# Zero-tile matmuls in TensorE's first waits, reordered loads, the expert number first on VectorE, and batch 0's routing moved into its own MoE stream

## The chip, the cores and the metric

The kernel runs on one core of a Trainium2 chip. A core has TensorE (PE, matrix multiplication; its weight loads are listed as PEld), VectorE (DVE), ScalarE (ACT), GpSimd (POOL), SyncE (SP, which here only issues DMAs) and 16 DMA engines. The metric is device time in microseconds (us) from start to end, as a median over runs. The profile is a record of one such execution.

## The reference

Attention twice over, then two mixture-of-experts (MoE) layers. Batch 8, 8 heads, 576 positions, head size 64, 32 packs; 512 model columns, 8 experts, hidden size 1024, all in float32.

```python
def sm_attn(qq, kk, vv):
    s = scale * np.matmul(qq, kk.transpose(0, 1, 3, 2))
    s = s - np.max(s, axis=-1, keepdims=True)
    a = np.exp(s)
    a = a / (np.sum(a, axis=-1, keepdims=True) + 1e-09)
    return np.matmul(a, vv)
p_packed = sm_attn(p, k, v)
x = sm_attn(q, p_packed, p_packed)      # then 4608 tokens x 512
...
expert_idx = np.argmax(x @ w_gate, axis=1)      # MoE 1
for e in range(E):
    h = np.maximum(x[mask] @ w1[e], 0.0)
    out[mask] = gate_w[mask, None] * (h @ w2[e])
...
# MoE 2: the same with a skip score: tokens with x @ w_skip <= 0 stay as they are
```

## The kernel before

Each batch runs through three generators of the attention: `gen_S` (scores s1 of the packs p against k, their maxima mx, the exponentials a, transposes at, the product pv with v, and the packed keys PKT), `gen_T` (scores s2 of q against PKT in two halves T0 and T1 of 288 positions, softmax along 32 packs, transposed back into A2; also the number e1i of the batch's main expert, from the key sums ks), and `gen_R` (gate logits L and the routing, whose gate rows gT go to DRAM and come back broadcast as gB).

MoE 1 then uses the batch's main expert. `gen_pre` loads that expert's W1 (four tiles of 512 KB, W1c; for batch 0 the last two lie in batch 0's result tile y), forms Q1 = PKT x W1 by matmuls q, and splits Q1 and A2 into a high and a low part (Q1h, Q1l, A2h, A2l) for three-product matmuls. `gen_w2` loads W2 (four tiles of 512 KB, W2c) and splits it into W2h (ACT) and W2l (DVE for tiles 0 and 2 of batch 0, else POOL). `gen_M` is the main stream of TensorE: for each half of the positions, `stage1` makes h in eight blocks of six matmuls (ACT writes hh, DVE writes hl from the same PSUM bank), and `stage2` makes y in four tiles of 24 matmuls; `sink` multiplies each y tile by gB on DVE. `stage2` reads the blocks in the order 3, 2, 1, 0, 7, 6, 5, 4, so the first 12 matmuls of a tile need blocks 0 to 3 alone.

Each engine's instructions stand in one fixed order, which is that in which the program issues them. `merge` takes turns among generators by a string of letters (`PAT`), and `Weave` lets side generators run between the steps of a main one: each side has a number of steps and a stretch of the main stream, as (generator, steps, from, to). Before batch 0's main stream, the attention of batch 0 and part of batch 1's `gen_S`, batch 0's `gen_T`, the first steps of `gen_pre` and `gen_w2`, then all of `gen_R(0)` and the rest of `gen_pre(0)` are issued. Batch 0's W2 tiles 2 and 3 are loaded when the tiles 0 and 1 have been split, since the pool `wcp` has two buffers. All PSUM tiles come from one ring of eight banks.

Of the kernel before, what the change touches and what calls it, by code (L numbers as in the profile page):

```python
# [9 lines left out]
F32 = mybir.dt.float32  # L10
# [12 lines left out]
F = 1024  # L23
# [8 lines left out]
PAT = (  # L32
    "ttpwaattttttppppppaaatttttta",
    "RRSRRRSRRRSRRRSRR",
# [84 lines left out]
def attn_moe_kernel(ctx, tc, q, k, v, p, wg, w11, w12, w21, w22, out):  # L119
# [213 lines left out]
    in_p = a_ctx.enter_context(tc.tile_pool(name="in_p", bufs=1))  # L333

    early_consts()

    st = [dict() for _ in range(B)]

    def load(b, nm, src, shape, parts, eng):
        t = in_p.tile([128] + shape, F32, tag=nm, name=nm, bufs=1 if nm == "v" else 2)  # L340
        eng = eng or (nc.sync,)
        for i, (dst, part_) in enumerate(parts(t, src[b]) if b == 0 else [(t, src[b])]):
            eng[i % len(eng)].dma_start(out=dst, in_=part_)
        st[b][nm] = t

    def quarters(t, a):
# [5 lines left out]

    def load_k(b, *eng):
        load(b, "pT", p, [128], lambda t, a: [(t, a)], eng[:1])
        load(b, "kT", k, [2, 4, HALF], quarters, eng)

    def load_v(b, *eng):
        load(b, "v", v, [9, 4, D], halves, eng)

# [3 lines left out]
    def heads(out, lhsT, rhs, **kw):  # L363
        for hp in range(4):
            for x in range(2):
                nc.tensor.matmul(  # L366
                    out=out[x][32 * hp:32 * hp + 32], lhsT=lhsT[64 * x:64 * x + 64, 32 * hp:32 * hp + 32],
                    rhs=rhs(hp)[64 * x:64 * x + 64], **kw,
                )

    def gen_S(b):
# [6 lines left out]
        for hf in range(2):  # L378
            s = [mt("s1")[:, 0:HALF] for _ in range(2)]
            s1.append(s)  # L380
            heads(s, pT, lambda hp: kT[:, hf, hp, :], start=True, stop=True)
# [27 lines left out]
        for x in range(2):  # L409
            for j in range(4):  # L410
                nc.tensor.transpose(ats[x][:, 128 * j:128 * j + 128], a1[:, x, 128 * j:128 * j + 128], ident)  # L411
            nc.scalar.copy(out=aT[:, 4 * x:4 * x + 4, :].rearrange("p j c -> p (j c)"), in_=ats[x])
# [39 lines left out]
    def gen_T(b):  # L452
# [12 lines left out]
        if b:  # L465
# [20 lines left out]
        for hf in range(2):  # L486
            T = Tt[hf]
            Tv = T.rearrange("p x (c e) -> p (x c) e", e=32)
            for x in range(2):
                nc.vector.transpose(out=T[:, x, :], in_=s2[hf][x][:, 0:HALF])  # L490
            yield
            mx2 = st_p.tile([128, 18], F32, name="mx2")
            nc.vector.tensor_reduce(out=mx2, in_=Tv, op=ALU.max, axis=AX.X)
            yield
            (nc.gpsimd if b == 0 and hf else nc.vector).tensor_tensor(
                out=Tv, in0=Tv, in1=mx2.unsqueeze(2).to_broadcast([128, 18, 32]), op=ALU.subtract
            )
# [12 lines left out]
            for x in range(2):  # L510
                nc.vector.transpose(out=A2[:, x, hf * HALF:(hf + 1) * HALF], in_=T[:, x, :])
            yield
# [52 lines left out]
    def split(hi, lo, x, eng):  # L565
        nc.scalar.copy(out=hi, in_=x)  # L566
        eng.tensor_tensor(out=lo, in0=x, in1=hi.bitcast(F32), op=ALU.subtract)  # L567

    def gen_pre(b):
# [108 lines left out]
    def gen_M(b, halves=(0, 1)):  # L678
# [171 lines left out]

    us[0]["y"] = bulk.tile([128, 4, S], F32, tag="y", name="y1", bufs=2)
# [395 lines left out]
    for b in range(B):  # L1247
# [328 lines left out]
```

## Time and profile before

| | us |
|---|---|
| median of 3 runs | 621.17 (620.44 to 621.42) |
| the profiled execution | 618.02 |
| its span, first to last instruction | 616.4 |
| PE busy of the span | 588.2 (95%) |
| DVE, ACT, POOL busy | 339.4, 213.3, 133.1 |
| mean granted TensorE clock | 0.986 |

A granted clock of 1.00 is the 2.4 GHz level, 0.50 the 1.2 GHz level. Times in a timeline are counted from the start of the span; the time of an instruction is from its start to its end, and neighbouring matmuls overlap, so that what one adds to a sequence is the distance of two starts.

### The profile page before, as it was taken

What the parts mean: (1) busy time and instruction counts of PE and PEld (TensorE: products, weight loads), DVE (VectorE), ACT (ScalarE), POOL (GpSimd) and SP (SyncE); (2) the same over time, 40 slices, a digit from 0 to 9 for tenths busy, and PEclk for the clock granted to TensorE, in tenths of its full rate; (3) what the DMA queues carried; (4) which work ended last, traced back from release to release, by engine and by line L of the source; (5) the groups of instructions that cost most, each with busy time, mean ns of one, the idle gap of its engine ahead of it and who ended that gap; (6) DMA issues with size and microseconds to landing.
All of it is one profiled execution on the core that took longest, in us unless ns stands there. A gap on an engine that the chain in (4) does not pass through costs nothing.

```text
span 616.4 us, 14334 instructions
## 1 busy us (share of the span) xinstructions
PE 588.2 (95%) x5737; PEld 529.2 (86%) x5738; DVE 339.4 (55%) x978; ACT 213.3 (35%) x463; POOL 133.1 (22%) x121
## 2 busy tenths in 40 slices
PE   4698999999999999999999999999999899999996
PEld 2287899899989989989988988799999899999796
DVE  2796738738737746845855854346656166253111
ACT  3352542442362343254244134215424135043110
POOL 3123151060150141132123114020301230140032
PEclk9698999999999999999999999999999999999998
DMA  8918788676477566637435415959137581732065
GB/s 341 346 56 311 282 305 325 224 255 240 175 253 252 211 238 237 252 113 283 177 100 216 178 60 191 342 117 401 33 111 281 76 356 27 236 58 113 1 92 64
DMA packets 35994, 122.18 MB, mean 198 GB/s; under 512 B 5696, under 2 KB 15680, under 8 KB 29888
## 3 DMA queue, kind: packets, MB, share of 16 engines
q1 hardware_dynamic: 30064, 113.56, 50.0%
q0 software_dynamic: 3968, 4.98, 6.4%
q10 hardware_dynamic: 1872, 2.49, 1.2%
q8 instruction: 50, 0.82, 0.5%
q14 instruction: 40, 0.33, 0.2%
HBM read 91.62 MB, written 29.39 MB: 196 GB/s over the span
## 4 chain that ended last, share of the span: by engine, by line
PE 68%; issue 11%; another core or an unknown queue 7%; DVE 5%; DMA 4%; POOL 2%; POOLq 1%; ACT 1%; SPq 0%; DVEq 0%; ACTq 0%
PE y L670 33%; PE h L649 18%; PE y L1225 4%; PE q L366 3%; PE s L366 3%; PE L L706 2%; DMA out_dram<-iXR 2%; POOL iW2l L567 1%; PE pv L422 1%; PE at L411 1%; DMA kT<-in_k_dram 1%; DMA W2c<-in_w_dram 1%; PE L L523 1%; DMA W1c<-in_w_dram 1%
## 5 line engine op out<-in xcount | busy, mean ns | idle before, releaser
L670 PE MATMUL y<-hh,W2h 128*128 128x288 f32 x512 | 156.5, 306 | 1.9 <-ACT W2h L566 1.9
L670 PE MATMUL y<-hh,W2l 128*128 128x288 f32 x512 | 151.5, 296 | 0.7 <-DVE W2l L567 0.7
L670 PE MATMUL y<-hl,W2h 128*128 128x288 f32 x512 | 151.8, 296 | 0.0
L670 PEld LDWEIGHTS y<-hh,W2h 128*128 128x128 f32 x512 | 97.0, 189 | 18.9 <-issue 13.5
L567 POOL TENSOR_TENSOR W2l<-W2c,W2h 128x1024 fp32r<-128x1024 f32 x30 | 72.4, 2413 | 156.5 <-ACT W2h L566 121.8
L670 PEld LDWEIGHTS y<-hh,W2l 128*128 128x128 f32 x512 | 97.0, 190 | 1.0 <-DVE W2l L567 1.0
L670 PEld LDWEIGHTS y<-hl,W2h 128*128 128x128 f32 x512 | 96.8, 189 | 0.1
L655 DVE SCALAR_TENSOR_TENSOR hl<-h,hh 128x288 fp32r<-128x288 f32 x128 | 57.9, 455 | 43.4 <-ACT hh L654 43.0
L654 ACT ACTIVATE hh<-h 128x288 fp32r<-128x288 f32 x128 | 52.6, 412 | 80.4 <-PE h L649 80.2
L649 PE MATMUL h<-A2h,Q1h 128*128 128x288 f32 x256 | 78.3, 306 | 0.0
L649 PE MATMUL h<-A2l,Q1h 128*128 128x288 f32 x256 | 75.5, 295 | 0.0
L649 PE MATMUL h<-A2h,Q1l 128*128 128x288 f32 x256 | 75.3, 294 | 0.0
L649 PE MATMUL h<-eXh,eW1h 128*128 128x288 f32 x192 | 57.8, 301 | 3.9 <-issue 3.3
L1225 PE MATMUL y<-ihh,iW2h 128*128 128x288 f32 x192 | 56.8, 296 | 0.0
L1225 PE MATMUL y<-ihh,iW2l 128*128 128x288 f32 x192 | 56.6, 295 | 0.0
L1225 PE MATMUL y<-ihl,iW2h 128*128 128x288 f32 x192 | 56.5, 294 | 0.0
L649 PE MATMUL h<-eXl,eW1h 128*128 128x288 f32 x192 | 56.5, 294 | 0.0
L649 PE MATMUL h<-eXh,eW1l 128*128 128x288 f32 x192 | 56.5, 294 | 0.0
L687 DVE TENSOR_TENSOR y<-y,gB 128x288 f32<-128x288 f32 x64 | 28.6, 447 | 44.7 <-PE y L670 42.1
L649 PEld LDWEIGHTS h<-A2h,Q1h 128*128 128x128 f32 x256 | 48.0, 187 | 3.8 <-issue 2.3
L566 ACT CAST W2h<-W2c 128x1024 fp32r<-128x1024 f32 x32 | 33.6, 1051 | 49.3 <-DMA W2c<-in_w_dram 19.5
L649 PEld LDWEIGHTS h<-A2h,Q1l 128*128 128x128 f32 x256 | 48.1, 188 | 0.0
(289 smaller groups left out, 948.7 us busy)
## 6 DMA issues: line engine op xcount, KB each, us to landing
W2c<-in_w_dram SPq DMA_DIRECT2D x32, 512.0 KB
eW<-in_w_dram SPq DMA_DIRECT2D x8, 2048.0 KB
W1c<-in_w_dram SPq DMA_DIRECT2D x30, 512.0 KB
kT<-in_k_dram SPq DMA_DIRECT2D x7, 1152.0 KB
qT<-in_q_dram SPq DMA_DIRECT2D x7, 1152.0 KB
v<-in_v_dram SPq DMA_DIRECT2D x7, 1152.0 KB
x2d<-y SPq DMA_DIRECT2D x7, 1152.0 KB
out_dram<-y SPq DMA_DIRECT2D x7, 1152.0 KB
```

What stands on the lines that cost most here:

```text
L366: nc.tensor.matmul(out=out[x][32 * hp:32 * hp + 32], lhsT=lhsT[64 * x:64 * x + 64, 32 * hp:32 * hp + 32], rhs=rhs(hp)[64 * x:64 * x + 64], ...
L411: nc.tensor.transpose(ats[x][:, 128 * j:128 * j + 128], a1[:, x, 128 * j:128 * j + 128], ident)
L422: nc.tensor.matmul(out=pv[x][32 * hp:32 * hp + 32], lhsT=aT[:, 4 * x + j, 32 * hp:32 * hp + 32], rhs=vm[:, 2 * hp + x, j, :], start=(j == ...
L566: nc.scalar.copy(out=hi, in_=x)
L567: eng.tensor_tensor(out=lo, in0=x, in1=hi.bitcast(F32), op=ALU.subtract)
L649: nc.tensor.matmul(out=ps[:, 0:nr], lhsT=l[:, t, 128 * f:128 * f + 128], rhs=r[:, t, :], start=(n == 0), stop=(n == 3 * kt - 1),)
L654: nc.scalar.activation(out=hh[:, f, :], in_=ps[:, 0:n_], func=ACTF.Relu)
L655: nc.vector.scalar_tensor_tensor(out=hl[:, f, :], in0=ps[:, 0:n_], scalar=0.0, in1=hh[:, f, :].bitcast(F32), op0=ALU.max, op1=ALU.subtract,)
L670: nc.tensor.matmul(out=ps[:, 0:HALF], lhsT=l[:, f, :], rhs=r[:, f, :], start=(n == 0), stop=(n == 23))
L687: nc.vector.tensor_tensor(out=y1[:, t, cols], in0=ps[:, 0:HALF], in1=d["gB"][:, cols], op=ALU.mult)
L706: nc.tensor.matmul(out=L[32 * i:32 * i + 32, 0:LN], lhsT=wgB[:, t, :], rhs=y1[:, t, LC[i]:LC[i] + LN], start=(t == 0), stop=(t == 3),)
L1225: nc.tensor.matmul(out=ps[:, 0:HALF], lhsT=l[:, f, 128 * t:128 * t + 128], rhs=r[:, f, c], start=(n == 0), stop=(n == 23))
```

## The change

It has five parts, all in the stretch of batch 0. (1) A tile `idle` of zeros, and groups of matmuls of it into a PSUM bank that nobody reads (`keep(n)`): 12 ahead of the first scores, 10 behind batch 0's s1, 3 between the transposes of its two row groups, 14 behind batch 1's s1. (2) k and then p of batch 0 are issued first, v only behind the first quarter of k, q behind v; batch 1's v behind batch 0's W2. (3) In batch 0's `gen_T` the four small operations that end in e1i stand first on DVE, T0 behind them, and T1 and half of batch 1's maxima behind T0's end. (4) All four W2 tiles of batch 0 are loaded at once, the last two into batch 1's result tile y. (5) `gen_R(0)`, the rest of `gen_pre(0)` and a new `gate0` are side streams of batch 0's main stream; its first half's y is copied from PSUM by ACT without the gate, and `gate0` multiplies by gB later, in SBUF.

```diff
+    idle = wk_p.tile([128, 512], BF16, name="idle")
+    nc.vector.memset(idle, 0.0)
+    def keep(n, ins=None):
+        with tc.issue_after(ins) if ins is not None else nullcontext():
+            ps = mt("keep")
+            for _ in range(n):
+                nc.tensor.matmul(out=ps, lhsT=idle[:, 0:128], rhs=idle, start=True, stop=True)
+    keep(12)
...
     def load_k(b, *eng):
+        ins = load(b, "kT", k, [2, 4, HALF], quarters, eng)
         load(b, "pT", p, [128], lambda t, a: [(t, a)], eng[:1])
-        load(b, "kT", k, [2, 4, HALF], quarters, eng)
+        return ins
...
+        if b < 2:
+            keep((10, 14)[b], last)
         for hf in range(2):
-            for x in range(2):
-                nc.vector.tensor_reduce(out=mx[:, x, hf:hf + 1], in_=s1[hf][x], op=ALU.max, axis=AX.X)
+            with tc.issue_after(st[0]["turned"]) if b == 1 and hf else nullcontext():
+                for x in range(2):
+                    nc.vector.tensor_reduce(out=mx[:, x, hf:hf + 1], in_=s1[hf][x], op=ALU.max, axis=AX.X)
...
+            if b == 0 and x == 0:
+                keep(3, last)
...
-            for x in range(2):
-                nc.vector.transpose(out=T[:, x, :], in_=s2[hf][x][:, 0:HALF])
+            with tc.issue_after(d["turned"] if hf else e1_ins) if b == 0 else nullcontext():
+                for x in range(2):
+                    nc.vector.transpose(out=T[:, x, :], in_=s2[hf][x][:, 0:HALF])
...
+        if early:
+            spare = us[1]["y"].rearrange("p t c -> p (t c)")
+            for t in (2, 3):
+                W.append(load_w2c(src, d["e1"], t, spare[:, F * (t - 2):F * (t - 1)].rearrange("p (f c) -> p f c", f=8)))
+            with tc.issue_after(hold[-1]):
+                load_v(1)
...
         def sink(hf, t, ps):
             cols = slice(hf * HALF, (hf + 1) * HALF)
+            if b == 0 and hf == 0:
+                nc.scalar.copy(out=y1[:, t, cols], in_=ps[:, 0:HALF])
+                return
...
+    def gate0():
+        d = us[0]
+        for t in range(4):
+            y = d["y"][:, t, 0:HALF]
+            nc.vector.tensor_tensor(out=y, in0=y, in1=d["gB"][:, 0:HALF], op=ALU.mult)
+            yield
...
-    load_k(0, nc.sync, nc.scalar)
-    load_v(0, nc.sync, nc.scalar)
+    k0 = load_k(0, nc.sync, nc.scalar)
     nc.scalar.dma_start(out=wgAB, in_=wg)
-    load_q(0, nc.sync, nc.scalar)
+    behind = mybir.DependencyInfo(mybir.DependencyClass.Sync, mybir.DependencyReason.DATA)
+    tc.add_manual_dep(load_v(0, nc.sync)[0], k0[0].name, behind)
+    with tc.issue_after(k0[2]):
+        load_q(0, nc.sync)
+        load_k(1)
+        load_q(1)
...
-    run_gen(gen_R(0))
-    run_gen(pre0)
...
                 sides.append((w20, 4, 0.0, 0.14))
+                sides.append((chain(gen_R(0), pre0, gate0()), 21, 0.14, 0.66))
```

The first place is DVE behind the key sums ks of batch 0. T_269 (T_298 in the changed kernel) is T0, T_270 (T_299) is T1, s_331 to s_342 (s_370 to s_381) are batch 1's scores s1. Before:

```order
L448 TENSOR_REDUCE ks<-kw 128x8
L490 STREAM_TRANSPOSE T_269<-s_272 128x288
L468 TENSOR_REDUCE mm<-s_271 128x1
L470 SCALAR_TENSOR_TENSOR ky<-s_271,mm,rev 128x8
L490 STREAM_TRANSPOSE T_269<-s_271 128x288
L474 TENSOR_REDUCE kmA<-ky 128x1
L493 TENSOR_REDUCE mx_355<-T_269 128x18
L475 TENSOR_SCALAR e1i<-kmA 32x1
L490 STREAM_TRANSPOSE T_270<-s_273 128x288
```

In the changed kernel, at the same place:

```order
L468 TENSOR_REDUCE ks<-kw 128x8
L488 TENSOR_REDUCE mm<-s_300 128x1
L490 SCALAR_TENSOR_TENSOR ky<-s_300,mm,rev 128x8
L494 TENSOR_REDUCE kmA<-ky 128x1
L495 TENSOR_SCALAR e1i<-kmA 32x1
L511 STREAM_TRANSPOSE T_298<-s_300 128x288
L511 STREAM_TRANSPOSE T_298<-s_301 128x288
L514 TENSOR_REDUCE mx_364<-T_298 128x18
```

Two transposes and one maximum that stood between ks and e1i stand behind e1i now.

The second place is DVE in the first half's h blocks of batch 0. The hl rows are blocks 0, then 1 to 3, then 4, then 5 to 7; W2l from W2c is tile 0 of W2, W2l from y_145 is tile 2, and A_338 is A2. In the changed kernel:

```order
L687 SCALAR_TENSOR_TENSOR hl<-h,hh 128x288
L524 TENSOR_SCALAR sm_475<-sm_475 128x18
L589 TENSOR_TENSOR W2l<-W2c,W2h 128x1024
L526 RECIPROCAL rc_478<-sm_475 128x18
L687 SCALAR_TENSOR_TENSOR hl<-h,hh 128x288 x3
L532 STREAM_TRANSPOSE A_338<-T_299 128x288 x2
L687 SCALAR_TENSOR_TENSOR hl<-h,hh 128x288
L589 TENSOR_TENSOR W2l<-y_145,W2h 128x1024
L687 SCALAR_TENSOR_TENSOR hl<-h,hh 128x288 x3
L589 TENSOR_TENSOR A2l<-A_338,A2h 128x576
```

and POOL, whose W2l rows are the tiles 1 and 3 and whose T_299 rows are T1:

```order
L516 TENSOR_TENSOR T_299<-T_299,mx_471 128x576 [waits DVE_49,Pool_49]
L589 TENSOR_TENSOR W2l<-W2c,W2h 128x1024 [waits DMAHW3_49,Activation_49]
L527 TENSOR_TENSOR T_299<-T_299,rc_478 128x576 [waits DVE_49,Pool_49]
L589 TENSOR_TENSOR W2l<-y_145,W2h 128x1024 [waits DMAHW5_49,Activation_49]
L527 TENSOR_TENSOR T_681<-T_681,rc_771 128x576 [waits DVE_49,Activation_49]
```

Before, POOL had the two T1 rows first and both W2l rows behind them, and DVE's second W2l stood far behind the last hl. Now the second W2l stands ahead of the last three hl on DVE, and a W2l stands between the two T1 operations on POOL.

The third place is SP behind the gate rows gm1d of batch 0 (gB is batch 0's, A_695 and A_721 are batch 1's A2). Before:

```order
L301 DMA gm1d<-gT 8x128
L623 ISA
L623 DMA gB<-gm1d 128x576
L562 ISA
L562 DMA W2c<-in_w_dram 128x1024
```

In the changed kernel:

```order
L301 DMA gm1d<-gT 8x128
L596 TENSOR_LOAD e1i
L596 ISA x2
L353 DMA kT<-in_k_dram 128x2304
L535 DMA a2d<-A_721 128x1152
L649 ISA
L649 DMA gB<-gm1d 128x576
```

The load of gB stands behind the store of batch 1's A2, which waits for batch 1's whole `gen_T`, and the multiplications of `gate0` stand among the second half's hl rows on DVE.

## Rows read from the trace of the kernel before

**Rows 1.** Busy us of PE, PEld, DVE, ACT, POOL by stretch; granted clock; DMA share; GB/s.

```profile
0.00:57.00 57.00, 39.08 (x508) 27.51 (x510) 37.43 (x121) 21.56 (x54) 13.36 (x50) 0.88 0.72 270
...
18.80:29.05 10.25, 6.31 (x84) 2.10 (x72) 8.46 (x26) 3.74 (x13) 1.16 (x1) 0.50 0.89 341
...
53.20:56.25 3.05, 3.05 (x13) 3.05 (x14) 3.05 (x5) 0.68 (x1) 2.86 (x1) 0.50 1.03 435
...
57.00:110.00 53.00, 52.85 (x570) 47.74 (x570) 34.55 (x104) 20.29 (x46) 14.45 (x8) 1.00 0.79 291
```

**Rows 2.** A wait of PE from 0 to 75 us: total, times, longest.

```profile
PE y L670 <- ACT W2h L566: 1.9, 1, 1.9
```

**Rows 3.** Timeline of PE, batch 0's attention to its first h: start, length, what, count.

```profile
8.33 1.22 PE L366 MATMUL s<-kT,pT 64*32 64x288 f32 x16 [1.07 <-DMA kT<-in_k_dram]
...
11.41 2.04 PE L411 MATMUL at<-ident,a 128*128 128x128 f32 x8 [1.86 <-ACT a L394]
...
13.59 1.93 PE L422 MATMUL pv<-v,aT 128*32 128x64 f32 x64
...
17.11 0.72 PE L366 MATMUL s<-qT,PKT 64*32 64x288 f32 x16 [0.35 <-ACT PKT L437]
...
25.16 3.09 PE L366 MATMUL q<-W1c,PKT 64*32 64x512 f32 x16 [3.94 <-DMA W1c<-in_w_dram]
...
30.33 0.40 PE L649 MATMUL h<-A2h,Q1h 128*128 128x288 f32 x1
```

**Rows 4.** Timeline of PE later: at, batch 0's second half, s of batch 2, y.

```profile
31.23 1.03 PE L411 MATMUL at<-ident,a 128*128 128x128 f32 x8
...
60.83 0.29 PE L649 MATMUL h<-A2h,Q1h 128*128 128x288 f32 x1
...
61.71 1.44 PE L523 MATMUL L<-A,gs 128*32 128x160 f32 x16
...
68.87 1.20 PE L366 MATMUL s<-kT,pT 64*32 64x288 f32 x32
...
70.24 0.30 PE L670 MATMUL y<-hl,W2h 128*128 128x288 f32 x1
...
73.17 0.29 PE L670 MATMUL y<-hh,W2l 128*128 128x288 f32 x1
```

**Rows 5.** Chain that ended last, 100 to 170 us: start, us, what.

```profile
135.84 1.03 PE pv L422 x64
...
159.60 0.68 PE L L523 x16
```

**Rows 6.** DMA from 0 to 60 us in 40 slices: GB/s.

```profile
GB/s 0 99 383 416 413 411 413 419 423 418 430 373 313 343 138 289 407 412 421 421 120 0 0 249 144 11 0 0 54 8 121 154 375 410 413 449 424 406 424 135
```

**Rows 7.** Timeline of DVE and SP: expert number, DMA issues, what waits for gB.

```profile
18.39 0.17 DVE L468 TENSOR_REDUCE mm<-s 128x1 f32<-128x8 f32 x1
...
19.91 0.13 DVE L475 TENSOR_SCALAR e1i<-kmA 32x1 int32<-32x1 f32 x1
...
21.08 0.89 SPq L584 DMA_DIRECT2D W1c<-in_w_dram  x2
...
44.11 0.39 SPq L623 DMA_DIRECT2D gB<-gm1d  x1
...
49.18 0.46 DVE L687 TENSOR_TENSOR y<-y,gB 128x288 f32<-128x288 f32 x1 [2.52 <-DMA gB<-gm1d]
...
62.66 0.34 SPq L513 DMA_DIRECT2D a2d<-A  x1
```

**Rows 8.** Timeline of DVE and POOL around a W2l of POOL.

```profile
35.07 1.18 DVE L567 TENSOR_TENSOR W2l<-W2c,W2h 128x1024 fp32r<-128x1024 f32 x1
...
37.61 2.38 POOL L567 TENSOR_TENSOR W2l<-W2c,W2h 128x1024 fp32r<-128x1024 f32 x1 [4.25 <-ACT W2h L566]
37.93 2.09 DVE L246 TENSOR_SCALAR s<-s 128x5 f32<-128x5 f32 x1
...
41.78 1.54 DVE L655 SCALAR_TENSOR_TENSOR hl<-h,hh 128x288 fp32r<-128x288 f32 x4
```

More of the change, by code (lines that the diff above doesn't have):

```diff
@@ L1 @@
-from contextlib import ExitStack
+from contextlib import ExitStack, nullcontext
 import concourse.bass as bass
@@ L32 @@
 PAT = (
-    "ttpwaattttttppppppaaatttttta",
+    "ttpwtttaatttppppppaaaatttttt",
     "RRSRRRSRRRSRRRSRR",
@@ L341, in load @@
         eng = eng or (nc.sync,)
-        for i, (dst, part_) in enumerate(parts(t, src[b]) if b == 0 else [(t, src[b])]):
-            eng[i % len(eng)].dma_start(out=dst, in_=part_)
+        ins = [
+            eng[i % len(eng)].dma_start(out=dst, in_=part_).ins
+            for i, (dst, part_) in enumerate(parts(t, src[b]) if b == 0 else [(t, src[b])])
+        ]
         st[b][nm] = t
+        return ins
     def quarters(t, a):
@@ L353, in load_k @@
     def load_k(b, *eng):
+        ins = load(b, "kT", k, [2, 4, HALF], quarters, eng)
         load(b, "pT", p, [128], lambda t, a: [(t, a)], eng[:1])
-        load(b, "kT", k, [2, 4, HALF], quarters, eng)
+        return ins
     def load_v(b, *eng):
-        load(b, "v", v, [9, 4, D], halves, eng)
+        return load(b, "v", v, [9, 4, D], halves, eng)
     def load_q(b, *eng):
@@ L365, in heads @@
             for x in range(2):
-                nc.tensor.matmul(
+                m = nc.tensor.matmul(
                     out=out[x][32 * hp:32 * hp + 32], lhsT=lhsT[64 * x:64 * x + 64, 32 * hp:32 * hp + 32],
@@ L369, in heads @@
                 )
+        return m.ins
     def gen_S(b):
@@ L380, in gen_S @@
             s1.append(s)
-            heads(s, pT, lambda hp: kT[:, hf, hp, :], start=True, stop=True)
+            last = heads(s, pT, lambda hp: kT[:, hf, hp, :], start=True, stop=True)
+        if b < 2:
+            keep((10, 14)[b], last)
         for hf in range(2):
-            for x in range(2):
-                nc.vector.tensor_reduce(out=mx[:, x, hf:hf + 1], in_=s1[hf][x], op=ALU.max, axis=AX.X)
+            with tc.issue_after(st[0]["turned"]) if b == 1 and hf else nullcontext():
+                for x in range(2):
+                    nc.vector.tensor_reduce(out=mx[:, x, hf:hf + 1], in_=s1[hf][x], op=ALU.max, axis=AX.X)
             yield
@@ L410, in gen_S @@
             for j in range(4):
-                nc.tensor.transpose(ats[x][:, 128 * j:128 * j + 128], a1[:, x, 128 * j:128 * j + 128], ident)
+                last = nc.tensor.transpose(ats[x][:, 128 * j:128 * j + 128], a1[:, x, 128 * j:128 * j + 128], ident).ins
+            if b == 0 and x == 0:
+                keep(3, last)
             nc.scalar.copy(out=aT[:, 4 * x:4 * x + 4, :].rearrange("p j c -> p (j c)"), in_=ats[x])
@@ L510, in gen_T @@
             for x in range(2):
-                nc.vector.transpose(out=A2[:, x, hf * HALF:(hf + 1) * HALF], in_=T[:, x, :])
+                last = nc.vector.transpose(out=A2[:, x, hf * HALF:(hf + 1) * HALF], in_=T[:, x, :]).ins
+            d["turned"] = last
             yield
@@ L565, in split @@
     def split(hi, lo, x, eng):
-        nc.scalar.copy(out=hi, in_=x)
-        eng.tensor_tensor(out=lo, in0=x, in1=hi.bitcast(F32), op=ALU.subtract)
+        a = nc.scalar.copy(out=hi, in_=x)
+        z = eng.tensor_tensor(out=lo, in0=x, in1=hi.bitcast(F32), op=ALU.subtract)
+        return a.ins, z.ins
     def gen_pre(b):
@@ L598, in halve @@
         def halve(hf):
-            split(d["A2h"][hf], d["A2l"][hf], A2[:, :, hf * HALF:(hf + 1) * HALF], nc.vector)
+            return split(d["A2h"][hf], d["A2l"][hf], A2[:, :, hf * HALF:(hf + 1) * HALF], nc.vector)
         Q1h = q1p.tile([128, 2, F], F32R, name="Q1h")
@@ L606, in gen_pre @@
             if b or n == 0:
-                halve(n)
+                cuts = halve(n)
             yield TE
@@ L614, in gen_pre @@
             for x in range(2):
-                split(Q1h[:, x, sl], Q1l[:, x, sl], ps[x], nc.vector)
+                with ExitStack() as order:
+                    for ins in cuts if b == 0 and n == 0 else ():
+                        order.enter_context(tc.issue_after(ins))
+                    split(Q1h[:, x, sl], Q1l[:, x, sl], ps[x], nc.vector)
                 yield
@@ L637, in gen_w2 @@
             split(W2h, W2l, W[t], nc.vector if early and t % 2 == 0 else nc.gpsimd)
-            if t + 2 < 4:
+            if t + 2 < 4 and not early:
                 W.append(load_w2c(src, d["e1"], t + 2))
@@ L849, in y_list @@
         yield
-    us[0]["y"] = bulk.tile([128, 4, S], F32, tag="y", name="y1", bufs=2)
-    load_k(0, nc.sync, nc.scalar)
-    load_v(0, nc.sync, nc.scalar)
+    us[0]["y"], us[1]["y"] = (bulk.tile([128, 4, S], F32, tag="y", name="y1", bufs=2) for _ in range(2))
+    k0 = load_k(0, nc.sync, nc.scalar)
     nc.scalar.dma_start(out=wgAB, in_=wg)
-    load_q(0, nc.sync, nc.scalar)
+    behind = mybir.DependencyInfo(mybir.DependencyClass.Sync, mybir.DependencyReason.DATA)
[4 more added lines that the diff above has]
+        load_q(1)
     warm = const.tile([128, 1], F32, name="warm")
@@ L866, in part @@
             yield said
-    load_all(1)
     S1 = gen_S(1)
@@ L1253, in attn_moe_kernel @@
                 sides.append((w20, 4, 0.0, 0.14))
+                sides.append((chain(gen_R(0), pre0, gate0()), 21, 0.14, 0.66))
             if b + 2 < B:
-                plan = ((NS if b else 7, 0.0, 0.19), (NT, 0.19, 0.5), (NR, 0.5, 1.0))
+                plan = ((NS, 0.0, 0.19) if b else (7, 0.06, 0.22), (NT, 0.19 if b else 0.22, 0.5), (NR, 0.5, 1.0))
             else:
```

4 lines of the change are left out of this document (2 added, 2 removed).

## Prediction

> **What bounds the kernel now.** I read the busy time by stretch first. From 57 us on TensorE is never short of work for long (52.85 of 53.00 us busy from 57 to 110 us, granted clock 1.00), but of the first 57 us it is busy 39.08, at a mean clock of 0.88 [rows 1]. So the kernel is bound by TensorE's main stream, and what can be won is how much earlier that stream gets through batch 0; whatever comes earlier by the end of batch 0's first y tiles stays won. The change touches nothing behind that point. The landmarks, in the order in which the reader meets them: s1 of batch 0 can begin its second half only at 8.33; s2 at 17.11; W1c is issued at 21.08 and the q matmuls wait 3.94 us for it, to 25.16; the first h is at 30.33 [rows 3, 7]; PE waits 1.9 us for W2h of tile 2, whose load was issued late [rows 2]; the second half's h begins at 60.83 and the first y tile of that half ends at 73.17 + 0.29 = 73.46 [rows 4]. Two pieces run at the half clock, 0.50: from 18.8 to 29.05, and from 53.20 to 56.25 behind the W2 wait; they use up the 0.12 that the mean lacks, (10.25 + 3.05) x 0.5 / 57, so all else is recorded at the full level [rows 1].
>
> **k first, and the zero matmuls: s2 earlier by 2.4.** k and p of batch 0 are 4 x 288 and 64 KB (the quarters of one 1152 KB tensor), 1.25 MB with kilobytes read as such and the wg tile behind. The DMA row has slices of 1.5 us: 0.15 + 0.57 + 0.62 MB, 1.34 MB, have moved by 6.0 us [rows 6]. Now part of that is v; with v behind k all of it is k and p. I take 7.0 for the last quarter (bounds 6.0, the bytes alone, and 8.33, no gain). The 12 zero matmuls start when the tile is set, near 1.4. The clock rows say only that PE ran at the half level behind its waits and was at the full one from 29.05, 3.9 us after it began on q without a gap at 25.16, and from 56.25, 3.05 us after 53.20 [rows 1, 3]. Ahead of 18.8 the record says full, but the lengths are those of the half level: 16 s matmuls in 1.22, where later 32 take 1.20 [rows 3, 4]; I go by the lengths. From 1.4 the zero matmuls fill 12 x 0.43 = 5.1 us at the half pitch (0.235 per 288 columns: 13 in 3.05 [rows 1], scaled to 512), so the clock should be up at about 5, and s1 runs 7.0 to 8.2. That is 1.35 ahead of 8.33 + 1.22 = 9.55, and the maxima and exponentials behind it follow as before. From there to s2, the transposes go at 1.03 instead of 2.04 and pv at 1.03 instead of 1.93 [rows 3 to 5]: 0.9 of pv in full, and of the transposes half, 0.5, since the first four await the exponentials. The 10 and 3 zero matmuls stand in waits (1.86 us of idle time stand ahead of the first transpose [rows 3]; ten at the full pitch of 0.133 x 512/288 = 0.235 [rows 4] are 2.35 us and may stick out by the difference). I take off 0.35 for that: s2 at 17.11 - 1.35 - 1.4 + 0.35 = 14.7.
>
> **Expert number first: W1c earlier by 3.2.** From mm to e1i it is 19.91 - 18.39 = 1.52 [rows 7]. Without the two transposes and the maximum between them, four dependent small operations are left; I take 0.75. The load then follows 1.17 behind e1i as now: 21.08 - 2.4 - 0.8 = 17.9. What covers this is the queue: k, p, wg, v and q of batch 0 and k, p, q of batch 1 are 6.2 MB, done at 6.0 + (6.2 - 1.34)/0.415 = 17.7 [rows 6], now without batch 1's 1.15 MB of v ahead; so W1c is at hand 25.16 - 21.08 = 4.1 later as before [rows 3, 7], at 22.0. The 14 zero matmuls (3.3 us) fill that wait, so that q need not begin at the half clock, as it did. From there DVE sets the pace, with T0, T1, Q1l and A2l in one line, so no more is won, and the first h is at 30.33 - 3.2 = 27.1.
>
> **W2 all at once, and what takes its place.** The W2 wait of 1.9 and the half clock behind it go. The half clock cost 13 x (0.235 - 0.133) = 1.3. All four tiles follow W1's four at 512 KB / 0.415 = 1.25 us each, the last near 30.7 and v behind it by 33.5: ahead of their users. But the splits that were spread over 25 us now meet. POOL has T1's subtraction, W2l of tile 1 (2.38 [rows 8]), T1's product (576 elements for 1024, 1.3), W2l of tile 3 (2.38), one behind another; ACT's W2h of tile 1 stands behind h's block 2, so POOL goes from about 33.4 to 39.5. DVE's line from T1 on (Q1l, T1's sums, W2l of tile 0, hl, A2), laid out by its rows' lengths, reaches W2l of tile 2 at 38.3, ahead of hl of blocks 5 to 7, and it meets POOL's W2l of tile 3. What such a meeting costs is in a pair of rows: DVE's 128x5 operation at 37.93, begun under POOL's W2l (37.61 + 2.38 = 39.99), took 2.09 and ended at 40.02 [rows 8]. So I take it that DVE's W2l of tile 2, ready at 38.3, does its 1.18 only behind 39.5: 40.7, and the three hl (1.54/4 = 0.385 each [rows 8]) end at 41.9. The lower bound is no meeting: 40.6. PE, whose h blocks go by DVE's hl through the ring of eight PSUM banks, has by then done h and pv (37.15) and 12 matmuls of the first y tile, which need blocks 0 to 3, at 38.8. The other 12 need blocks 4 to 7: PE idles 3.1 us, 38.8 to 41.9.
>
> The Trainium skill ("SBUF — State Buffer", section "SBUF: two separate sides") states that DVE and GpSimd share a pair of ports as an exclusive lock, held for the whole instruction by whichever starts first, where the DVE one has two SBUF inputs. By that rule the tile-2 split waits its full share, as above, and the kernel comes out at 617.3; by the lower bound it comes out at 616.0. The 2.09 us of [rows 8] agree with the rule.
>
> From 41.9: 12 y (1.6), L, ps, PKT, s2, wg and the key sums of batch 1 at full speed (3.5, with two short waits), and the other 72 y matmuls at (73.17 - 70.24)/22 = 0.133 [rows 4], 9.6: the second half's h begins at 56.6, 4.2 earlier.
>
> **gB late: 1.2 lost.** y of the first half no longer waits for gB, since ACT copies it; nothing waits for ACT there. But gB's load now stands on SP behind the store of batch 1's A2. From gB's issue at 44.11, about when batch 1's scores came, to the store of that A2 at 62.66 it was 18.55, with DVE's wait for gB of 2.52, the W2 wait of 1.9, DVE's split of 1.18 and POOL's of 2.38 in it [rows 2, 7, 8]; that leaves 10.6, from s2 at 46.9 to 57.5; gB issues at 58.0 and lands 49.18 - 44.11 = 5.07 later [rows 7], 63.1. Behind gB on DVE, in one line, stand four products of gate0 and eight hl of the second half, 12 x 0.385 = 4.6: the last hl at 67.7. PE needs it at 66.5 (h with L 7.2, where L is 0.68 of 1.44 since its waits shrink [rows 4, 5], s1 of batch 2 1.2 and 12 y 1.6 behind 56.6): 1.2 idle. Now from 60.83 to 73.46 is 12.63; less 0.6 of L, plus 1.2, the y tile ends at 69.6.
>
> **Sum.** 73.46 - 69.6 = 3.9 us. Against the profiled execution, 618.02 (span 616.4 and 1.6 around it), that is 614.1; that execution was 3.15 under the median of the runs, 621.17, and a gain is carried to the median: **617.3**. The other edits cost nothing that shows: 39 more matmuls lie in waits, ACT's four copies in its idle time, four products on DVE are counted with gB.
>
> **Rivals.**
> (a) The clock falls in the new 3.1 us idle stretch. It did so behind 1.9 and 0.7 us of idle (the half clock from 53.20). That costs the same 1.3: 618.6. Against it: PE is busy without long gaps up to 38.8, and the clock rose by 29.05 before [rows 1].
> (b) The splits don't meet, or gB comes early, since batch 1's gen_T has little against it: 1.3 and 1.2 of the two stalls vanish, one or both: 616.0 to 614.8; with PE's h also earlier than the DVE line lets me think, 613.6.
> (c) The gain is swallowed: k isn't there by 7.0 but at 8.3 (1.25), gB is later by as much as batch 1's k, q, W1 and v traffic delays it (up to 2 us, at DMA rates that stand above 400 GB/s in 18 slices of [rows 6]): 3.9 - 3.3 leaves 620.6.
> (d) Slower: the zero matmuls do not raise the clock. Then they are not free, for they stand ahead of real work at 0.43 each: ten end at 8.6 + 4.3 = 12.9 or later with the cold s1, three more 1.3 behind the first transposes, so s2 comes at 20.2 instead of 14.7, and W1c with it, 5.5 later: 622.8. It decides from 3.9 us of standing in the way; for it speaks that no row shows what a matmul of zeros does to the granted clock; against it, that full rows of any kind raised it at 29.05 and 56.25.
>
> **How the numbers follow.** Forecast 617.3: 0.36. (a) 618.6: 0.24. (b) 613.6 to 616.0: 0.22. (c) 620.0 to 621.5: 0.10. (d) above 622: 0.08. A measurement of this kernel tells about 0.2%, 1.24 us, from no change, so faster means under 619.9. The forecast, (a) and (b) are faster, 0.82; (c) lies mostly within 0.2%, 0.10; (d) is slower, 0.08. The range leaves out the tail of (b) below 613.6 and (d) and half of (c): 613.6 to 620.5.
>
> **What would show it.** Right: the first s matmuls near 7 us with 32 in 1.2; s2 under 15.5; W1c issued at 17 to 18.5; no PE wait for W2h; a PE wait for hl near 39 to 42 with DVE's W2l lengthened under POOL's; DVE waiting for gB near 60 to 63; the second half's h at 56 to 57.5. Wrong: zero matmuls at 0.43 beyond 6 us, PE waits for hl over 5 us, or gB's chain ending after 69.

## The result, and the profile after

The changed kernel takes 615.14 us (median of 4 runs, 613.70 to 616.69), the kernel before 621.19 (620.44 to 621.42): a ratio of 0.9895, 95% interval 0.9874 to 0.9916, 6.05 us less. The forecast was 617.3, range 613.6 to 620.5, a gain of 3.9. The profiled execution of the changed kernel took 616.69 (span 615.0), that of before 618.02 (616.4): in the two traces lie only 1.4 us, so each step has to be read in its own place.

Timeline of PE after, batch 0 up to its first h (start, length, what, count, in brackets the idle time ahead and what ended it); it answers to [rows 3].

```profile
7.18 1.21 PE L380 MATMUL s<-kT,pT 64*32 64x288 f32 x32 [1.19 <-DMA pT<-in_p_dram]
...
12.52 1.21 PE L442 MATMUL pv<-v,aT 128*32 128x64 f32 x64
...
15.30 0.72 PE L380 MATMUL s<-qT,PKT 64*32 64x288 f32 x16 [0.35 <-ACT PKT L457]
...
22.66 1.78 PE L380 MATMUL q<-W1c,PKT 64*32 64x512 f32 x16
25.86 1.71 PE L380 MATMUL q<-y,PKT 64*32 64x512 f32 x16 [1.42 <-DVE T L511]
27.50 0.40 PE L681 MATMUL h<-A2h,Q1h 128*128 128x288 f32 x1
```

All 32 s matmuls take 1.21, so the clock is up; s2 stands at 15.30 (17.11 before), the first h at 27.50 (30.33).

The same engine further on, around the wait for hl and in the second half; it answers to [rows 4].

```profile
38.27 0.29 PE L702 MATMUL y<-hh,W2h 128*128 128x288 f32 x1
41.54 0.40 PE L702 MATMUL y<-hl,W2h 128*128 128x288 f32 x1 [2.98 <-DVE hl L687]
...
42.76 0.44 PE L702 MATMUL y<-hh,W2h 128*128 128x288 f32 x1
...
56.93 0.29 PE L681 MATMUL h<-A2h,Q1h 128*128 128x288 f32 x1
...
70.36 0.29 PE L702 MATMUL y<-hh,W2l 128*128 128x288 f32 x1
```

PE stands idle for 2.98 us, and from 42.76 a y matmul takes 0.44 instead of 0.29. The first y tile of the second half ends at 70.65, 2.81 ahead of before. DVE and POOL in that wait, answering to [rows 8]:

```profile
36.93 2.38 POOL L589 TENSOR_TENSOR W2l<-y,W2h 128x1024 fp32r<-128x1024 f32 x1 [0.42 <-ACT W2h L588]
...
37.65 2.74 DVE L589 TENSOR_TENSOR W2l<-y,W2h 128x1024 fp32r<-128x1024 f32 x1
40.31 1.17 DVE L687 SCALAR_TENSOR_TENSOR hl<-h,hh 128x288 fp32r<-128x288 f32 x3
```

DVE's split takes 2.74 instead of 1.18 to 1.23: POOL's instruction ends at 36.93 + 2.38 = 39.31, and DVE's ends 1.08 behind that.

SP after, DMA issues; the first and third rows answer to [rows 7].

```profile
18.42 0.89 SPq L607 DMA_DIRECT2D W1c<-in_w_dram  x2
...
57.82 0.36 SPq L535 DMA_DIRECT2D a2d<-A  x1
58.52 0.35 SPq L649 DMA_DIRECT2D gB<-gm1d  x1
...
70.46 0.37 SPq L353 DMA_DIRECT2D qT<-in_q_dram  x1
70.93 0.38 SPq L353 DMA_DIRECT2D kT<-in_k_dram  x1
71.70 1.28 SPq L607 DMA_DIRECT2D W1c<-in_w_dram  x2
```

And what PE waits for behind it:

```profile
80.56 3.10 PE L380 MATMUL q<-W1c,PKT 64*32 64x512 f32 x16 [2.30 <-DMA W1c<-in_w_dram]
```

Here is a new loss. The second pair of batch 1's W1c tiles is issued behind q of batch 3 and k of batch 4, 1152 KB each, and PE can begin on them only at 80.56, 8.9 us later. It waits 2.30 and then runs q in 3.10, where it took 1.09 before. That is 4.3, more than all that batch 0 had won. Granted clock after, by stretch (busy us of PE, PEld, DVE, ACT, POOL; then clock, DMA share, GB/s), answering to [rows 1]:

```profile
0.00:57.00 57.00, 47.67 (x574) 33.13 (x578) 37.94 (x126) 23.04 (x58) 15.08 (x52) 0.97 0.78 301
57.00:110.00 53.00, 50.15 (x529) 42.52 (x528) 30.91 (x97) 19.22 (x46) 11.67 (x6) 0.97 0.73 271
42.76:46.20 3.44, 3.08 (x37) 1.67 (x44) 0.90 (x5) 0.67 (x2) 0.00 (x0) 0.52 1.00 410
80.50:83.80 3.30, 3.24 (x17) 0.63 (x18) 0.00 (x0) 0.08 (x1) 0.00 (x0) 0.53 0.98 381
```

In these stretches behind the two waits the granted clock is 0.52 and 0.53, the half level. What is left of the front is read in the chain of work that ended last: the first q of batch 2, before and after (two kernels, a fence each).

```profile
122.03 1.02 PE q L366 x16
```

```profile
123.60 1.02 PE q L380 x16
```

At batch 2 the changed kernel is 1.57 us *behind*. From there the streams are alike for some 200 us, up to a wait of 0.47 near 339 us after. Then comes the program's last part, the items of single experts, which begin behind branches. There, before has a wait that has no counterpart after. Timeline of PE before, at the branch into the second item:

```profile
491.12 0.37 PE L649 MATMUL h<-eXh,eW1h 128*128 128x288 f32 x1 [2.67 <-issue]
```

"issue" means that the engine waited for no instruction of another engine and no load of data that the profile shows. So two questions are open: what the front is worth, and what the change, which touches nothing there, has to do with this wait.

### The profile page after: what moved, and what is told of

Its sections match the earlier page's. It is cut to its first block, busy times and chain, and to the rows that moved or that the text cites. A ratio compares the mean times of both kernels' runs of the same rounds, so it can differ in the third digit from the quotient of the medians.

```text
span 615.0 us, 14410 instructions
## 1 busy us (share of the span) xinstructions
PE 595.0 (97%) x5774; PEld 531.6 (86%) x5777; DVE 336.5 (55%) x979; ACT 214.4 (35%) x467; POOL 132.1 (21%) x121
## 4 chain that ended last, share of the span: by engine, by line
PE 69%; issue 11%; DMA 7%; another core or an unknown queue 7%; DVE 3%; POOL 1%; SPq 1%; POOLq 0%; ACT 0%; DVEq 0%
PE y L702 32%; PE h L681 19%; PE y L1268 4%; PE q L380 3%; PE s L380 3%; PE L L748 2%; DMA out_dram<-iXR 2%; DMA W2c<-in_w_dram 1%; DMA W1c<-in_w_dram 1%; PE pv L442 1%; PE at L429 1%; DMA gB<-gm1d 1%; DMA out_dram<-ero 1%; PE L L545 1%
## 5 line engine op out<-in xcount | busy, mean ns | idle before, releaser
L589 POOL TENSOR_TENSOR W2l<-W2c,W2h 128x1024 fp32r<-128x1024 f32 x29 | 69.4, 2396 | 149.2 <-ACT W2h L588 131.7
L1268 PE MATMUL y<-ihh,iW2h 128*128 128x288 f32 x192 | 56.8, 296 | 0.0
L1268 PE MATMUL y<-ihh,iW2l 128*128 128x288 f32 x192 | 56.6, 295 | 0.0
L722 DVE TENSOR_TENSOR y<-y,gB 128x288 f32<-128x288 f32 x60 | 26.8, 447 | 41.3 <-PE y L702 39.2
L681 PEld LDWEIGHTS h<-A2l,Q1h 128*128 128x128 f32 x256 | 48.1, 188 | 0.0
```

What stands on the lines that cost most here:

```text
L589: z = eng.tensor_tensor(out=lo, in0=x, in1=hi.bitcast(F32), op=ALU.subtract)
L681: nc.tensor.matmul(out=ps[:, 0:nr], lhsT=l[:, t, 128 * f:128 * f + 128], rhs=r[:, t, :], start=(n == 0), stop=(n == 3 * kt - 1),)
L1268: nc.tensor.matmul(out=ps[:, 0:HALF], lhsT=l[:, f, 128 * t:128 * t + 128], rhs=r[:, f, c], start=(n == 0), stop=(n == 23))
```

## The experiments

All compute the full reference. The kernel before ran beside them; it took 621.2 to 621.9 as a median in each group. The ratios are to it.

**The changed kernel again**, unaltered.

> The changed kernel once more, for a second profile and more times. Theory A (the spread of the changed kernel, 613.7 to 616.7, is the granted clock: it falls behind the 3.0 us wait for hl and behind the 2.3 us wait for W1c of batch 1, or it does not): runs near 613.8 have a mean granted clock of 0.998 or more, runs near 616.5 one of 0.993 to 0.995; nothing in between. Rival B (the spread is instruction fetch late in the program, as the 2.7 us issue wait at 491 us of the kernel before): times spread at one and the same mean clock. Median 613.7 to 616.7 by both.

618.12 (615.70 to 619.19), ratio 0.9930 (0.9908 to 0.9952), in another group of runs. That is 3.27 below before, where the first group had 6.05; their intervals just overlap, and the difference stays unexplained. Theory A fails as put: times near 618 and 619 have no place in it. But the clock goes with the time: the two shortest, 615.70 and 616.20, have a mean clock of 0.996 and 0.995, the other four 0.992 or 0.993, so rival B, one and the same clock, fails too. The profile shows the same two waits, hl 3.0 and W1c 3.0, and the first q of batch 2 at 125.36.

**Without the zero matmuls.**

```diff
     def keep(n, ins=None):
+        return
```

> The changed kernel without its 39 zero matmuls, all else as it is. Theory (they buy the full clock in the attention of batch 0: pv at 1.21 instead of 1.93 us, half of the transposes' 1.0, and q at 1.8 instead of 3.1 us): s2 at 16.4 instead of 15.3, first h 1 to 2 us later, so 616 to 618.5. Rival (DVE's line sets when h can go on, and the clock that PE has ahead of it does not matter): s2 later by 1, but the second half's h later by under 0.5, and 615 to 615.6.

621.12, ratio 0.9986 (0.9967 to 1.0005): no longer faster than before, and outside both expectations. The front does not say why. s2 is at 17.23 and the first h at 31.59, yet the second half's h is at 57.23 against 56.93 and 57.38 in the two profiles with them, under the rival's 0.5. The 4 us are made up at the splits: DVE's takes 1.92 here, PE has no wait for hl, and the clock is 1.00 from 38 to 50 us. The first q of batch 2, at 123.85, lies between 123.53 and 125.36 with them. The profile has the wait at the branch again (waits of PE over the span: total, times, longest):

```profile
PE h L682 <- issue: 3.9, 2, 3.3
```

**p ahead of k again from batch 1 on.**

```diff
     def load_k(b, *eng):
+        if b:
+            load(b, "pT", p, [128], lambda t, a: [(t, a)], eng[:1])
         ins = load(b, "kT", k, [2, 4, HALF], quarters, eng)
-        load(b, "pT", p, [128], lambda t, a: [(t, a)], eng[:1])
+        if not b:
+            load(b, "pT", p, [128], lambda t, a: [(t, a)], eng[:1])
```

> The changed kernel with p ahead of k again for the batches from 1 on (k first for batch 0 alone). On SP this moves the 1152 KB load of a later batch's k from ahead of the second pair of batch 1's W1c tiles to behind gB. Theory (W1c landed 8.7 us after its issue, since k and q of later batches lay ahead of it in the queue, 2.3 MB or 5.6 us at 415 GB/s; PE waited 2.3 us and then ran q at the half clock, 3.1 instead of 1.1): the wait goes, 2.3 to 4.3 us less, 611 to 612.8. Rival (the time is given back at the next wait, for instance hl or the next loads): 614 to 616.5 as now.

613.82 (612.44 to 614.76), ratio 0.9865 (0.9844 to 0.9886), 4.3 below the changed kernel in the same group. SP, DMA issues of this kernel:

```profile
72.09 0.37 SPq L353 DMA_DIRECT2D qT<-in_q_dram  x1
72.57 0.38 SPq L353 DMA_DIRECT2D pT<-in_p_dram  x1
73.76 0.94 SPq L610 DMA_DIRECT2D W1c<-in_w_dram  x2
81.90 0.33 SPq L652 DMA_DIRECT2D gB<-gm1d  x1
82.28 0.43 SPq L353 DMA_DIRECT2D kT<-in_k_dram  x1
```

k stands behind the W1c tiles now, and PE has no wait for them. The order of p and k, changed for batch 0 and with it for all batches, was the cause of that loss. The time lies between the two expectations, which were made from the first group's times; against the changed kernel beside it, the gain is the theory's. By batch 2 its trace shows 1.3 of it against the first profile of the changed kernel, and 3.1 against the second.

**W2l of tile 2 on POOL.**

```diff
-            split(W2h, W2l, W[t], nc.vector if early and t % 2 == 0 else nc.gpsimd)
+            split(W2h, W2l, W[t], nc.vector if early and t == 0 else nc.gpsimd)
```

> The changed kernel with W2l of tile 2 of batch 0 on POOL instead of DVE, so that it no longer stands ahead of the last three hl. Theory (the 3.0 us idle time of PE at 38.3 is the lock between DVE's split, 2.74 instead of 1.2, and POOL's): PE's wait for hl falls below 0.6, the clock does not fall at 42.6, and the second half's h begins 2.5 to 4 us earlier: 611 to 612.8. Rival 1 (POOL's line becomes the bound: W2l of tiles 2 and 3 end at 39 and 41.5, needed at about 44 and 47): a wait for W2l, gain under 1. Rival 2 (the gain is swallowed by gB or by W1c of batch 1): h at 54 but the time within 0.7 of 615.

613.85 (613.28 to 615.41), ratio 0.9880 (0.9861 to 0.9899), 4.3 below the changed kernel. POOL and DVE in this kernel:

```profile
36.72 5.26 POOL L589 TENSOR_TENSOR W2l<-y,W2h 128x1024 fp32r<-128x1024 f32 x2
```

```profile
37.56 1.51 DVE L687 SCALAR_TENSOR_TENSOR hl<-h,hh 128x288 fp32r<-128x288 f32 x4
```

The hl, which read one operand from PSUM, run beside POOL's splits at their usual 1.5 for four; PE's wait for hl is 0.28, the clock stays up, and the second half's h begins at 53.26, 3.7 earlier. W1c is waited for 2.84 all the same, so the two losses are separate.

**Both.**

> The changed kernel with both: p ahead of k for the batches from 1 on, and W2l of tile 2 on POOL. Theory (the wait for hl, 3.0 us and a fall of the clock, and the wait for W1c of batch 1, 2.3 to 3.0 us and a fall of the clock, are two separate losses): both gains add up, 4.3 + 4.3 below the changed kernel, ratio to before 0.980 to 0.983, 609 to 610.5. Rival (both end in one and the same later wait): 612.5 to 613.8, as with either alone.

610.27 (608.63 to 610.62), ratio 0.9824 (0.9799 to 0.9848). The gains add up, and it beats both kernels. PE's waits in this kernel between 30 and 120 us, all of them:

```profile
PE s L383 <- DVE hl L690: 0.8, 1, 0.8
PE s L383 <- ACT PKT L460: 0.4, 1, 0.4
PE pv L445 <- DMA v<-in_v_dram: 0.3, 1, 0.3
PE y L705 <- DVE hl L690: 0.2, 1, 0.2
```

**The kernel before again**, for its branch wait.

> The kernel before once more, for a second profile. If the 2.7 us in which PE waits for nothing that the profile shows, at the branch into the second expert item near 490 us, belong to the program (theory L: the distance from the first instruction to that branch target decides how its code is fetched), they stand there again, 2 to 3.5 us. If they are chance (rival), they are absent or elsewhere. Time 619 to 624; the first q matmuls of batch 2 at 122 to 125.5, which is the front's part of the spread.

620.99, ratio 1.0007 (0.9985 to 1.0029). The wait is there again, longer:

```profile
493.35 0.58 PE L649 MATMUL h<-eXh,eW1h 128*128 128x288 f32 x1 [3.39 <-issue]
```

**Before, with 39 one-column zero matmuls at the start.**

```diff
+    idle = wk_p.tile([128, 128], BF16, name="idle")
+    nc.vector.memset(idle, 0.0)
+    pad = mt("keep")
+    for _ in range(39):
+        nc.tensor.matmul(out=pad[:, 0:1], lhsT=idle, rhs=idle[:, 0:1], start=True, stop=True)
     early_consts()
```

> The kernel before with 39 zero matmuls of one column at its start, ended before k is there: nothing else is moved, but PE's branches come as many instructions later as in the changed kernel. Theory L: the wait at the branch near 490 us goes, and the time is 2.5 to 3.5 less than that of before, 618 to 619. Rival (the zero matmuls of the changed kernel won their time by the clock, in batch 0): as before within 0.7, 620.7 to 622.

614.69 (613.30 to 616.42), ratio 0.9898 (0.9873 to 0.9922). None of the change's parts is in this kernel, only its 78 more PE instructions (39 weight loads, 39 matmuls) ahead of the branches, and it is as much faster as the changed kernel was in its first group: 6.75 below before, over twice what theory L had expected. The only wait of PE from 430 to 550 us:

```profile
PE h L654 <- ACT ex L286: 1.5, 1, 1.5
```

**The changed kernel with one-column zero matmuls.**

```diff
-                nc.tensor.matmul(out=ps, lhsT=idle[:, 0:128], rhs=idle, start=True, stop=True)
+                nc.tensor.matmul(out=ps[:, 0:1], lhsT=idle[:, 0:128], rhs=idle[:, 0:1], start=True, stop=True)
```

> The changed kernel with its 39 zero matmuls cut to one column each, in the same places: the same number of instructions, next to no work. Theory L (what the zero matmuls won, 621.1 - 618.1 on one chip, was the branch wait of 3.3 us): the time of the changed kernel within 1, 3 below that without them; the branch wait absent; s2 and the first h of batch 0 as without them. Rival (the clock in batch 0): the time of the kernel without them, 0.3 below before.

619.86, ratio 0.9972 (0.9949 to 0.9994). In the profile the branch wait is gone, as theory L has it, but the time is only 1.3 below the kernel without zero matmuls, not 3: the front is later here (first q of batch 2 at 126.41, for 123.85). DVE's split takes 2.75, PE waits 3.0 for hl, and the second half's h is at 58.62, 1.2 and 1.7 later than with the full ones, so what the splits made up without zero matmuls was not the rule. The time is 1.7 above the changed kernel, with the two intervals just overlapping. A miss on the number; the front of this kernel varies by as much as what was to be told apart.

**7 and 32 of them instead of 39, in the kernel before** (14 and 64 PE instructions).

> The kernel before with 7 one-column zero matmuls at its start (14 more PE instructions with their weight loads, where 39 were 78). Theory L64 (what counts is the place of the branch target within a block of 64 instructions: 14 and 78 differ by 64): the branch wait near 490 us is absent, first item 53.1 us from its first h to that of the second, and 614 to 616. Rival Lfar (a shift of 14 is too small, or the place counts in another unit): wait of 2.7 to 3.4 us, 56.8 to 57.6 from item to item, 620.5 to 622. Rival P (early work of PE itself, or the tile that the pad takes in PSUM, makes the gain): between, 616 to 620.

> The kernel before with 32 one-column zero matmuls at its start, 64 more PE instructions: a whole block by theory L64, and nearly the same early work as with 39. Theory L64: the wait near 490 us stays, item to item 56.8 to 57.6, 620.5 to 622. Rivals P (the early work) and Lfar (any large shift does it): as with 39, item to item 53.1, 614 to 616.

With 7: 617.87, ratio 0.9945 (0.9929 to 0.9960). With 32: 613.95, ratio 0.9882 (0.9864 to 0.9901). Theory L64 falls twice: 64 instructions do all that 78 do, 14 about half. No period of 64. The 617.87 lies in rival P's range. The PSUM tile of the pad is the same with 7, 32 and 39, so it cannot make the difference among them; early work is tested below.

**Both mended places, with one-column zero matmuls.**

> The kernel with both mended places (p ahead of k from batch 1 on, W2l of tile 2 on POOL), its 39 zero matmuls cut to one column each. It tells what their work, the clock alone, is worth at equal code places. Theory (s1, transposes, pv and q at the half clock: the first h 2 to 3 us later, and nothing behind it gives that back): 612 to 613.5. Rival (DVE's line hides it): 610 to 611.

611.40, ratio 0.9845 (0.9824 to 0.9865), against 0.9824 (0.9799 to 0.9848) with the full ones. The first h is 1.64 later (29.11 for 27.47), the second half's h 1.74 (54.81 for 53.07), the first q of batch 2 1.33 (117.95 for 116.62): nothing behind it gives it back, as the theory has it. The time lies between the two expectations. What the work of the zero matmuls, and so the clock ahead of the first h, is worth is 1.1 us by the medians, less than the two intervals can tell from nothing, and 1.3 to 1.7 by the two traces.

**Before, with the 39 in the middle of the program**, ahead of batch 3's main stream.

```diff
+    idle = const.tile([128, 128], BF16, name="idle")
+    nc.vector.memset(idle, 0.0)
...
+        if b == 3:
+            pad = mt("keep")
+            for _ in range(39):
+                nc.tensor.matmul(out=pad[:, 0:1], lhsT=idle, rhs=idle[:, 0:1], start=True, stop=True)
         if b < B - 1:
             W = Weave(gen_M(b), NM, sides)
```

> The kernel before with 39 one-column zero matmuls in the middle of the program, ahead of batch 3's main stream and some 1,500 PE instructions ahead of the first branch. Batch 0 is untouched. They stand in a stretch in which PE is the bound, so they cost what they take, 1 to 2.5 us. Theory L (the branches come 78 instructions later): from the first h of the first expert item to that of the second 53.1 to 54.4 us instead of 56.8 to 57.6, the wait near 490 us absent, and 615 to 617.5. Rival P (what the pads did came from work of PE at the start, or from what they held up there): 56.8 to 57.6, the wait there, and 621.5 to 623.5.

616.59 (615.69 to 619.38), ratio 0.9928 (0.9903 to 0.9953). Batch 0 is untouched and nothing early is done; the pads cost 1.0 where they stand:

```profile
L1270 PE MATMUL keep<-idle x39: 163/163/167, 184.0 to 185.0; 128*128 128x1 bf16 x39
```

and the wait at the branch is absent. So it is the instructions ahead of the branch that matter, not early work.

The traces side by side, from starts of matmuls: first q of batch 2; from it to the first h of the first item; from that to the second item's; from that to the third's; and the span.

| kernel | more PE instructions | q of batch 2 | to item 1 | to item 2 | to item 3 | span |
|---|---|---|---|---|---|---|
| before | 0 | 121.96 | 312.37 | 56.79 | 51.51 | 616.4 |
| before, again | 0 | 123.29 | 312.45 | 57.61 | 52.92 | 620.0 |
| without zero matmuls | 0 | 123.85 | 312.49 | 57.63 | 53.41 | 621.1 |
| before + 7 | 14 | 123.48 | 312.31 | 55.18 | 51.69 | 616.4 |
| before + 32 | 64 | 122.34 | 312.02 | 54.35 | 50.88 | 613.4 |
| before + 39 | 78 | 122.26 | 313.83 | 53.11 | 50.88 | 613.8 |
| before + 39 in the middle | 78 | 122.51 | 315.42 | 53.10 | 50.88 | 615.6 |
| the change | 78 | 123.53 | 313.78 | 53.10 | 50.88 | 615.0 |
| the change, again | 78 | 125.36 | 314.46 | 53.12 | 50.88 | 617.5 |
| the change, one column | 78 | 126.41 | 313.42 | 53.11 | 50.88 | 617.5 |
| loads in order | 78 | 122.24 | 313.16 | 53.09 | 50.88 | 613.1 |
| tile 2 on POOL | 78 | 119.82 | 314.28 | 53.08 | 50.88 | 611.7 |
| both | 78 | 116.62 | 313.51 | 53.09 | 50.88 | 607.8 |
| both, one column | 78 | 117.95 | 313.95 | 53.11 | 50.88 | 609.7 |

The two columns of the items go by the instruction count: with 78 they agree within 0.03, whatever the kernel. What the change and its mendings do to the front is in the third column.

*What the wait at the branch ends on.* PE's own branch instructions into the second and the third item, before:

```profile
L1499 PEldq COMPARE_BRANCH  x1: 3583/3583/3583, 487.0 to 487.0; - x1
...
L1504 PEldq COMPARE_BRANCH  x1: 2678/2678/2678, 539.7 to 539.7; - x1
```

And in the changed kernel:

```profile
L1543 PEldq COMPARE_BRANCH  x1: 349/349/349, 489.0 to 489.0; - x1
...
L1548 PEldq COMPARE_BRANCH  x1: 348/348/348, 538.9 to 538.9; - x1
```

They take 3.58 and 2.68 us before, 0.35 after. Within each of the two long ones the DMA view of before lists one transfer of the kind "instruction" on queue q8; the row for the first, 487.05 to 490.63 us:

```profile
q8 instruction: 1, 0.02, 1.7%
```

Each transfer of q8 is one block of 16 KB, 49 or 50 in each profile. They are PE's, by number: PE lists some 11,600 instructions (an estimate of 235 per block), no other engine much over 1,100. In the four profiles with 0 or 14 instructions more, the block lands 0.4 to 3.1 us after PE's branch has begun, and the branch ends 1.31 to 1.36 (second item) and 1.51 (third) after the landing. In the ten with 64 or 78, the last block landed 2.9 to 5.1 us ahead of the branch, which takes 0.34 to 0.36. So PE waits there for its own instructions. The other waits put down to "issue" go the same way: all 23 of 0.18 us and more, in the 14 profiles, end 1.2 to 2.0 us after such a block has landed. One of 0.36 to 0.53 between 332 and 342 us is in the kernels with 64 or 78 alone, and the branch into the first item, 0.34 with up to 64, takes 0.74 to 1.27 with 78: that is where the fourth column grows.

## Why the prediction was right, and where it was not

The time came out near the forecast by luck. The account of it was right in kind up to 70 us and wrong behind that: what batch 0 won was lost again by batch 2, and the measured gain came from behind the branches, where none was forecast.

*k first and the zero matmuls.* k and p were at hand at 7.18 for 7.0, s1 was warm, s2 at 15.30 for 14.7. Right in kind, 0.6 short: s1 ended at 8.39 for 8.2, and from there to s2 it was 7.56 before and 6.91 after, 0.65 gained for 1.05. The transposes are where it went: from the first of them to the first pv 2.18 became 2.03, 0.15 less for 0.5. (A zero matmul at the half pitch is 0.42 by the row that the prediction scales, not 0.43; that moves little.)

*Expert number first.* W1c was issued at 18.42 for 17.9, 2.66 earlier than before, and the first h came at 27.50 for 27.1.

*The splits that meet.* Forecast: DVE's split held to POOL's end, PE idle from 38.8 to 41.9. Found: 38.56 to 41.54. The Trainium skill ("SBUF — State Buffer", section "SBUF: two separate sides") has the shared ports as a lock held for a whole instruction; the 2.74 us split agrees, and so do the unslowed hl beside POOL, which have one operand in SBUF and one in PSUM. With tile 2 on POOL the wait fell to 0.28; there DVE's A2l, with two operands in SBUF, began at 39.00, ahead of POOL's second split at 39.08, kept its 0.75, and POOL's split took 2.90 for 2.41. The 2.09 us operation that the prediction reads with the rule has one input, in SBUF, and so is not a case of the two inputs that it names.

*Rival (a).* The clock did fall behind that wait, to 0.52 from 42.76 to 46.20, though the forecast gave it 0.24. In the profile of the loads in order it was at 0.62 over 38 to 50 us, and the second half's h came at 59.88.

*gB.* Issued at 58.52 for 58.0; DVE took it up at 64.59, 6.07 later where 5.07 was taken, and the y tile ended at 70.65 for 69.6. By the prediction's own terms, 56.6 + 12.63 - 0.6 + 1.2, it ends at 69.8, which makes the forecast gain 3.6. Found to that point: 2.81, with the clock of rival (a) and gB's later landing against it.

*The step that failed* is in the first paragraph: "whatever comes earlier by the end of batch 0's first y tiles stays won. The change touches nothing behind that point." Both halves are wrong. First, `load_k` now issues k ahead of p in every batch, and with it k of batch 4 stood ahead of batch 1's second W1c pair on SP: 2.3 of waiting and 2.0 of half clock, which turned 2.81 won into 1.57 lost at batch 2. Undoing it gave back 4.3 in the time. The prediction followed the instructions of batch 0 through SP's queue and not those of later batches. Second, 78 more PE instructions stand ahead of every later branch of PE, the block of instructions that PE had waited for there had landed before the branch, and the items behind the branches got shorter: 4.3 (56.79 + 51.51 to 53.10 + 50.88) against the first profile of before, 6.6 against the second, with 1.3 to 1.4 lost between batch 2 and the first item. Against the second profile of before, 620.0, the change's 615.0 is 0.24 of front lost, 1.33 lost to item 1, 4.51 and 2.04 won behind it. That is 5.0 in these two traces, of 6.05 between the medians, and none of the rivals had it. Rival (c), the gain swallowed, was what happened to the front, with another queue entry than the ones it named.

That the zero matmuls are what makes the change faster is thus true by count far more than by clock: without them the ratio is 0.9986, while one-column ones in the old kernel give 0.9898. The work of the full ones, and so the clock, is worth 1.1 us by the medians of the mended kernel and 1.7 by those of the changed one, either hardly clear of noise.

Open: why PE's block is late with 0 or 14 instructions more and in time with 64 or 78. No run has more than 78, so whether the gain goes again with further ones is not known. Also open is how much of the front the unprofiled runs kept; the two shortest of the four, 613.70 and 613.90, have a mean clock of 0.999 and 0.998 against 0.995 and 0.993, so in them the clock seems not to have fallen.

## What to carry to other kernels

When a change adds or removes instructions ahead of a branch, compare the parts of the two traces that it doesn't touch, first of all the waits put down to "issue" behind branches, the length of the branch instruction itself and the transfers of the kind "instruction", before crediting it with the time; a padded copy of the old kernel is the control. When a load's order is changed in a helper that all rounds use, follow it through the queue in all rounds: a prefetch that nobody is waiting for yet can stand ahead of one that somebody is. And a split that is moved to fill a gap should be looked at with the engine that shares its ports: beside POOL's split, four hl with an operand in PSUM took their usual 1.5 us, while a split with both operands in SBUF took 2.74 for 1.2 and left PE idle for 3.

## What the runs showed of the hardware that was not expected

14, 64 or 78 PE instructions more, of next to no work, shortened the two stretches behind PE's late branches from 56.8 to 57.6 us down to 55.2, 54.4 and 53.1, and the following one from 51.5 to 53.4 down to 51.7, 50.9 and 50.9. A branch of PE took 0.34 to 0.36 us where its last 16 KB block of instructions had landed 2.9 us or more ahead, and 1.7 to 4.4 where the block landed within it, ending 1.3 to 1.5 after the landing. Ahead of 18 us the granted clock is recorded as 1.00 in every profile but that of the loads in order (0.97), while the 32 s matmuls take 2.17 without zero matmuls or with one-column ones, and 1.21 with the full ones.
